# Chunks 1 and 4 in row Pairs ahead of the first down stage, chunk 2's second norm transposed by DMA, eleven half tiles, row copies on VectorE: one change to an adaLN block

## The chip, the cores and the metric

One core of one Trainium2 chip. The metric is the device time of one execution of the program in microseconds (us), median over runs.

## The reference, cut to what matters

An adaLN block on x of 2048 rows by D = 576 columns, bf16: local dilated attention of 32 heads of 18 columns, then a gated MLP of width F = 4608, each behind a layer norm that is scaled and shifted by vectors made from a condition c, and each added to x through a gate.

```python
# sa, ca, ga, sb, cb, gb = the six blocks of silu(c) @ w_mod
h = layernorm(x) * (1 + ca) + sa
q, k, v = split(h @ wqkv)
# row s looks at rows s, s-2, ..., s-14; softmax over these 8, per head
o = softmax((q . k[s - 2w]) * 18**-0.5, over w) . v[s - 2w]
x = x + ga * (o @ wo)
h = layernorm(x) * (1 + cb) + sb
x = x + gb * (((h @ w_gate) * (h @ w_up)) @ w_down)
```

## The kernel before, in words

The rows are cut into eight chunks of 256. The MLP runs over groups of chunks, GROUPS = [[0], [1, 2], [3, 4], [5, 6], [7]] (L42). For each group there is a gate/up stage and then a down stage. Everything else, that is the attention and both norms of later chunks, is threaded between the matmuls of these stages.

*Gate/up.* The 4608 columns are 36 f tiles of 128, loaded in nine blocks of four (`load_wgu`, SP's queue, three rotating buffers). One f tile is a `Pair` (L772): TensorE's 128 rows are used as two halves of 64 contraction rows, the gate product on one half and the up product on the other, and then the halves swap banks. `first` of a Pair is put ahead of `second` of the Pair before it. ScalarE (ACT) evicts both products as u_sb and g_sb, VectorE (DVE) multiplies them into hh (L815 for a half tile, L824 for a full one). In the second gate/up stage (chunks 1 and 2) the first HEAD = 8 f tiles are each split into "f0" (chunk 1's columns) and "f1" (chunk 2's), so that the stage can begin before chunk 2's second norm is ready; the f1 tiles need the mark "h2". A new weight block is asked for at f = 4, 8, ... of the f1 or full tiles.

*Down.* The 36 tiles of hh are multiplied with w_down's blocks (`load_wd`, GpSimd's queue), 128 by 512 and 128 by 64 per row tile, into one bank per row tile and a shared one. Weight blocks 5 and 6 of the first stage are put in prod_t's space (`ld_prods`, L1332).

*Attention.* For each chunk: `a_ln` and its norm, the transposition into hT (on TensorE, or by DMA on SP's queue, `a_td`, L417), modulation by DVE or ACT, q and k (`a_q` unpaired, `qk_pair` L827 as a Pair), v (`a_v` or `v_pair` L850), rows of v written to DRAM scratch vd and read back shifted as vsh (`b_ld`, L475, GpSimd's queue), products of q and shifted k (`b_p`), logits summed per head on TensorE (`b_l`), softmax, weighting and adding (`b_mul`, `b_add`), o into oT (`b_o` on TensorE, `b_od` by DMA), the output projection (`b_w`, L653, unpaired; `w_pair`, L873, as two Pairs). Then the second norm (`b_ln`, `b_norm`) and its transposition into h2T (`b_t`, L680, ten TensorE transposes; `b_td`, L685, two DMA transposes), modulated afterwards (`b_mod`).

A Pair for attention contracts 576 = 4 × 128 + 64 rows; the last 64 must stand in both halves of the partitions. For the weights this is a copy of 64 rows into the other 64: `both_halves` (L1323: wqk 1152 columns, wv 576) and `wo_both` (L870: wo 576), both on GpSimd. For hT and oT it is a doubled last tile: the norms of chunks 3, 5, 6 and 7 also write 64 columns behind the 576 (`both`), and `o_tail` (L550) fills the same columns of o. PAIRED = (3, 5, 7) lists the chunks whose output projection is a Pair.

*What sets the order.* All engines run in the order of the program. That order is worked out when the kernel is built, by `timed` (L893): it goes through the f tiles with a clock of planned times, and after each tile puts in the pieces of several threads whose marks are due, and at most one extra Pair from a list. In the tables `gbg` (L1362) and in `first_down` (L1375), an entry is (TensorE time, DVE time, marks needed, mark given, delay of that mark, call). Around the change, before:

- In the first gate/up stage (chunk 0): extra Pairs are q, k and v of chunk 3; threads are chunk 3's and 4's first norm and the attention of chunks 1 and 2. `both_halves` is called behind the MLP's gate row.
- In the first down stage: chunk 4's ten transposes, chunk 1's ten o transposes, chunk 4's q and k in five groups and v in two, chunk 1's output projection, all unpaired; then chunk 1's second norm (by DMA transposes), chunk 2's values and its output projection.
- In the second gate/up stage: chunk 2's second norm is transposed on TensorE among the f0 tiles; both vsh loads of chunk 3, its residual rows and `wo_both` come first; then chunk 5's norm and chunk 3's and 4's attention.

Of the kernel before, what the change touches and what calls it, by code (L numbers as in the profile page):

```python
# [18 lines left out]
P = 128  # L19
# [22 lines left out]
GROUPS = [[0], [1, 2], [3, 4], [5, 6], [7]]  # L42
PAIRED = (3, 5, 7)


@with_exitstack
def kernel(
# [279 lines left out]
    def transposed(src, dst, cols, vi):  # L327
        n = P * len(cols)
        pA = ps([P, 3, n], BF, "tr_pA")
        pB = ps([P, 2, n], BF, "tr_pB")  # L330
        for m in range(KT):
            d = pA[:, m, :] if m < 3 else pB[:, m - 3, :]
            for c, j in enumerate(cols):
                nc.tensor.transpose(d[:, js(c)], src[:, j, m * P:(m + 1) * P], ident[:])

        def evict(first_on_dve=True):
            for m in range(KT):
                s = pA[:, m, :] if m < 3 else pB[:, m - 3, :]
                modulate(dst(m), s, m, vi + 1, vi, (m < 3) == first_on_dve)
        return evict  # L340
# [81 lines left out]
    def a_t4():  # L422
        a_t(4, False)
        nc.gpsimd.memset(aa[4]["hT"][64:, KF, :], 0.0)

# [49 lines left out]
    def b_ld(i, j):  # L475
        b = bb.setdefault(i, dict(prod={}, vsh={}))
        base = HALO + i * CH + j * P - DIL * (W - 1)
        vsh = vshp.tile([P, W, DH, H], BF, name="vsh")
        vsrc = bass.AP(vd.tensor, vd.offset + base * D, [[D, P], [DIL * D, W], [1, D]])
        b["vsh"][j] = vsh  # L480
        return nc.gpsimd.dma_start(vsh[:].rearrange("p w d h -> p w (d h)"), vsrc)  # L481

# [200 lines left out]


    def b_td(i):  # L685
        ht, o0 = h2_of(i)
        xn = bb.pop(i)["xn"]
        for j in range(ST):
            nc.sync.dma_start_transpose(out=ht[:, :, o0 + j * P:o0 + (j + 1) * P], in_=xn[:, j, :])

# [34 lines left out]
    def values_of(i, nxt=None):  # L725
        r = []
        for j in range(ST):
            r += [(0, 0.75, f"a{i}", "-", 0, lambda j=j, w=w: b_mul(i, j, w)) for w in range(0, W, 2)]
            r += [(0, 0.75, "", "-", 0, lambda j=j: b_add(i, j, 0)), (0, 0.75, "", "-", 0, lambda j=j: b_add(i, j, 1)),
                  (0, 1.2, "", f"o{i}{j}", 0, lambda j=j: b_add(i, j, 2))]  # L730
            if i in PAIRED:
                r.append((0, 0, "", f"O{i}" if j == ST - 1 else "-", 11.0 if i == 7 else 14.0, lambda j=j: b_od(i, (j,))))
# [137 lines left out]
    def wo_both():  # L870
        nc.gpsimd.tensor_copy(wo[64:, KF, :], wo[0:64, KF, :])

# [18 lines left out]
    QKP = [(0, 1), (2, 3), (4,), (5, 6), (7, 8)]  # L891

    def timed(items, extra, threads, slack, busy=0.0):  # L893

        t, dve = 0.0, busy
        done, seq = {f"v{i}": 0.0 for g in GROUPS for i in g[1:]}, []
        done["late"] = 0.0
        extra, threads = list(extra), [list(th) for th in threads]

# [17 lines left out]
        for kind, f, step, own, need in items:  # L917
# [11 lines left out]
            t += step  # L929
        assert not extra, (extra[0][1], t)  # L930
        return seq, [(*p[0:2], p[2] if all(x in names(th) for x in p[2].split()) else "late", *p[3:]) for th in threads for p in th]

# [11 lines left out]

    HEAD = 2 * FB

# [39 lines left out]
    def wgu_spaces():  # L986
        for k, space in ((3, value_space()), (4, value_space()), (8, prod_t)):
# [3 lines left out]

    WD_ASKS = [{0: (7,), 1: (8,), 2: (9,), 7: (10,)},
# [330 lines left out]
    def both_halves():  # L1323
        for w_t, n in ((wqk, 2 * D), (wv, D)):
            nc.gpsimd.tensor_copy(w_t[64:, KF, 0:n], w_t[0:64, KF, 0:n])

# [32 lines left out]
    first.pop(at)  # L1359
    at = [k for k, p in enumerate(first) if p[3] == "o11"][0] + 2  # L1360
    first.insert(at, (0, 0, "o11", "O1", 0, nop))
    gbg = {0: (qkv_of(3, "p17 z3"),  # L1362
               [[(0, 0, "", "-", 0, lambda: (load_wm5(), load_wd(0))), (0, 0, "", "z3", 8.0, nop), (0, 0, "", "w5", 12.0, nop), (0.85, 0, "w5", "-", 0, gb_row), (0, 0, "", "-", 0, lambda: (load_res(2), both_halves()))],
                norm_of(3, "", "", 5) + [(0, 2.5, "", "m4", 0.2, lambda: a_ln(4)), (0, 0, "m4", "r4", 1.0, lambda: aa[4]["rsq"]()),
                                         (0, 0, "r4", "e4", 2.0, lambda: aa[4]["norm"]((0,))), (0, 0, "e4", "n4", 1.6, lambda: aa[4]["norm"]((1,))),
                                         (0, 0, "n4 v3", "x4", 0, nop)],
               first, [(0, 0, "y1", "s1", 0.6, lambda: b_exp(1))]]),
           1: (qkv_of(5, "p37") + wo_of(3),
               [[(0, 0, "", "-", 0, lambda: (loads_v(3), load_res(3), load_res(4), wo_both()))], norm_of(5, "p33", "", 7), second]),
           2: (qkv_of(6, "") + wo_of(5),  # L1370
# [3 lines left out]

    def first_down(late):  # L1375
        def q(g):
            return (0.53 if g == 2 else 1.07, 0, "h4", "-", 0, lambda: a_q(4, g))

        def v(j):
            return (1.2, 0, "h4", "-", 0, lambda: a_v(4, j))  # L1380

        def out_1(first):
            return [(0, 0, "", "o0", 0.4, nop), (0.55, 0, "o0", "o1", 1.9, lambda: b_o(1)), (1.2, 1.35, "o1", "-", 0, lambda: b_w(1, 0)), (1.2, 1.35, "", "x1", 0.5, lambda: b_w(1, 1)),
                    (0, 2.5, "", "s1", 0.7, lambda: b_ln(1)), (0, 0, "s1", "n1", 2.3, lambda: b_norm(1)), (0, 0, "n1", "t1", 9.5, lambda: b_td(1)),
                    (0, 1.0, "t1", "-", 0, lambda: (b_mod(1, (3, 4), False), b_mod(1, (0, 1, 2), True)))]
        assert not {"O1", "x4"} & set(names(late))
        a4 = [(0.6, 0, "", "h4", 1.7, lambda: (a_t4(), load_x(6), ld_prods(0)))]
# [19 lines left out]
    for gi, grp in enumerate(GROUPS):  # L1407
# [15 lines left out]
        else:  # L1423
            left = down(gi, hh, first_down(late) if gi == 0 else next_down(gi, late))
            assert gi == 0 or not left
# [30 lines left out]
```

## Time and profile before

| what | us |
|---|---|
| median of three runs | 539.52 |
| lowest and highest | 539.25 to 539.95 |
| the profiled execution | 541.99 |
| its span | 539.7 |

The profile is of one execution of its own; its span leaves out what lies before the first and behind the last recorded instruction. Its first part gives each engine's busy time, its second the span in 40 slices, its third the DMA queues (q0 are GpSimd's, q1 SP's and ACT's). The chain is followed back from the last instruction to what released each one. In timelines a row is: start, duration, engine, line, operation, output<-input, shapes, count, and in brackets the idle time before it with what ended it.

### The profile page before, as it was taken

How to read it: one execution, taken by the hardware profiler on the slowest of the kernel's cores; microseconds unless marked ns; L12 is line 12 of the kernel's file. 1: busy time of each engine (PE TensorE's matmuls, PEld its weight loads, DVE VectorE, ACT ScalarE, POOL GpSimd, SP SyncE). 2: the span in 40 equal slices, each digit the busy share in tenths (PEclk: the TensorE clock that was granted, in tenths of full speed). 3: DMA queues.
4: the chain of work that ended last, by engine and by line, in shares of the span. 5: the costliest groups of instructions: out<-in, count | busy, mean ns of one | idle time of the engine just before them, and what ended most of it. 6: DMA issues, size and time to landing. Idle time of an engine off the chain costs nothing.

```text
span 539.7 us, 14692 instructions
## 1 busy us (share of the span) xinstructions
PE 531.5 (98%) x6214; PEld 324.0 (60%) x6244; DVE 319.5 (59%) x731; ACT 252.8 (47%) x620; POOL 73.1 (14%) x113
## 2 busy tenths in 40 slices
PE   8999999999999999999999999999999999999997
PEld 4777889756755444555544454555544454558875
DVE  5898797759767788627467797504517733032212
ACT  4866877644656553112655543104555542006630
POOL 8104023112000110111000010110010101110210
PEclk9999999999999999999999999999999999999999
DMA  9999999979863871998445944983396694759731
GB/s 273 292 242 363 346 278 321 322 128 326 279 181 90 237 229 28 264 273 299 130 130 145 302 149 108 238 237 111 94 279 184 158 312 81 233 138 292 259 96 38
DMA packets 94659, 114.47 MB, mean 212 GB/s; under 512 B 27873, under 2 KB 83378, under 8 KB 94466
## 3 DMA queue, kind: packets, MB, share of 16 engines
q1 hardware_dynamic: 82864, 66.92, 45.7%
q0 software_dynamic: 11424, 46.40, 27.5%
q8 instruction: 49, 0.80, 0.7%
q10 hardware_dynamic: 306, 0.21, 0.1%
q14 instruction: 16, 0.13, 0.1%
HBM read 103.07 MB, written 4.74 MB: 200 GB/s over the span
## 4 chain that ended last, share of the span: by engine, by line
PE 97%; DMA 1%; issue 1%; DVE 0%; SPq 0%; ACT 0%
PE pg L770 29%; PE pu L770 23%; PE acc L1007 19%; PE pq L442 4%; PE pq L770 3%; PE accr L1012 3%; PE acc L1062 3%; PE pv L770 2%; PE pv L465 2%; PE lgT L499 2%; PE pw L659 2%; DMA wmA<-in_w_mod_dram 1%; PE pw L770 1%; PE po L614 1%; PE pwj L636 0%
## 5 line engine op out<-in xcount | busy, mean ns | idle before, releaser
L770 PE MATMUL pg<-h2T,wgu 64*128 64x512 bf16 (+1 forms) x1376 | 266.0, 331 | 0.0
L770 PE MATMUL pu<-h2T,wgu 64*128 64x512 bf16 (+1 forms) x1376 | 265.5, 331 | 0.0
L770 PEld LDWEIGHTS <-wgu 64*128 64x128 bf16 x2752 | 136.5, 94 | 93.3
L821 ACT CAST u_sb<-pu 128x512 bf16<-128x512 f32 (+1 forms) x172 | 85.4, 497 | 152.4 <-PE pg L770 150.4
L824 DVE TENSOR_TENSOR hh<-g_sb,u_sb 128x512 bf16<-128x512 bf16 x136 | 59.2, 435 | 114.1 <-ACT g_sb L822 113.1
L822 ACT CAST g_sb<-pg 128x512 bf16<-128x512 f32 (+1 forms) x172 | 86.8, 505 | 0.0
L1007 PEld LDWEIGHTS <-hh 128*128 128x128 bf16 x504 | 49.0, 98 | 59.3 <-issue 1.5
L1007 PE MATMUL acc<-wd,hh 128*128 128x512 bf16 x327 | 84.1, 380 | 0.1
L1012 PE MATMUL accr<-wd,hh 128*128 128x64 bf16 x344 | 62.4, 193 | 0.8
L770 PE MATMUL pu<-h2T,wgr 64*128 64x512 bf16 (+1 forms) x188 | 61.4, 327 | 0.0
L770 PE MATMUL pg<-h2T,wgr 64*128 64x512 bf16 (+1 forms) x188 | 61.4, 327 | 0.0
L1012 PEld LDWEIGHTS <-hh 128*128 128x128 bf16 x504 | 45.8, 98 | 1.2
L175 POOL DMA_DIRECT2D wd<-in_B_w_down_dram x29 | 21.8, 751 | 176.2 <-PE accr L1012 142.0
L548 DVE TENSOR_TENSOR vsh<-vsh,attn 128x1152 bf16<-128x1152 bf16 x56 | 39.7, 750 | 0.0
L487 DVE TENSOR_TENSOR prod_t<-qT,kT 128x1280 bf16<-128x1280 bf16 x36 | 28.2, 817 | 4.5 <-ACT kT L841 2.7
L770 PEld LDWEIGHTS <-wgr 64*128 64x128 bf16 x376 | 19.6, 94 | 15.1 <-issue 2.7
L1007 PE MATMUL acc<-prod_t,hh 128*128 128x512 bf16 x108 | 27.7, 380 | 0.0
L481 POOL DMA_DIRECT2D vsh<-vd x14 | 12.5, 896 | 96.6 <-DVE o_sb L556 76.1
L770 PE MATMUL pq<-hT,wqk 64*128 64x256 bf16 (+1 forms) x360 | 22.9, 259 | 0.0
L442 PE MATMUL pq<-hT,wqk 128*128 128x256 bf16 (+1 forms) x225 | 21.7, 251 | 0.1
L1012 PE MATMUL accr<-prod_t,hh 128*128 128x64 bf16 x112 | 21.6, 193 | 0.2
L325 ACT ACTIVATE h2T<-h2T,modc 128x256 bf16<-128x256 bf16 x12 | 6.5, 591 | 31.4 <-DMA h2T<-xn 31.4
(225 smaller groups left out, 628.3 us busy)
## 6 DMA issues: line engine op xcount, KB each, us to landing
wgu<-in_B_w_gate_dram SPq DMA_DIRECT2D x41, 512.0 KB, 4.8
wgu<-in_B_w_up_dram SPq DMA_DIRECT2D x41, 512.0 KB, 6.5
wd<-in_B_w_down_dram POOLq DMA_DIRECT2D x29, 576.0 KB, 5.2
vsh<-vd POOLq DMA_DIRECT2D x14, 1152.0 KB, 8.8
prod_t<-in_B_w_down_dram POOLq DMA_DIRECT2D x8, 576.0 KB, 5.9
hh<-in_B_w_down_dram POOLq DMA_DIRECT2D x6, 576.0 KB, 6.8
x_t<-in_A_x_dram SPq DMA_DIRECT2D x8, 288.0 KB, 5.3
x_r<-in_A_x_dram SPq DMA_DIRECT2D x8, 288.0 KB, 8.5
```

Of the source, the lines that this page charges most:

```text
L175: return nc.gpsimd.dma_start(wb[:], B_w_down[r0:r0 + FB * P, :].rearrange("(k p) n -> p k n", p=P))
L442: nc.tensor.matmul(pq[:, gi, :], lhsT=wqk[:, kt, m * P:(m + 1) * P], rhs=hT[:, kt, cols], start=(kt == order[0] and not (by_k and gi)), st ...
L481: return nc.gpsimd.dma_start(vsh[:].rearrange("p w d h -> p w (d h)"), vsrc)
L487: nc.vector.tensor_tensor(prod, aa[i]["qT"][:], aa[i]["kT"][:, :, off:off + CH], ALU.mult)
L548: nc.vector.tensor_tensor(v, v, at, ALU.mult)
L770: return nc.tensor.matmul(out, lhsT=lhs, rhs=rhs, start=first, stop=last, skip_group_check=True)
L821: nc.scalar.copy(u[:, c, :], pu)
L822: nc.scalar.copy(g[:, c, :], pg)
L824: return lambda: nc.vector.tensor_tensor(hh[:, f - c:f + 1, :], g, u, ALU.mult)
L1007: nc.tensor.matmul(acc[j][:], lhsT=hh[:, f, js(j)], rhs=wb[:, f % FB, 0:512], start=(f == 0), stop=(f == FT - 1))
L1012: nc.tensor.matmul(accr[:, j, :], lhsT=hh[:, f, js(j)], rhs=wb[:, f % FB, 512:D], start=(f == 0 and j == 0), stop=(f == FT - 1), skip_grou ...
L1062: nc.tensor.matmul(acc[i][:], lhsT=hh[:, f, js(j)], rhs=wb(f)[:, c0:c1], start=(f == 0), stop=(f == FT - 1))
```

## The change

- PAIRED gets chunk 1: its output projection becomes two extra Pairs at the end of the first gate/up stage. Its ten o transposes, and chunk 4's ten hT transposes, are put ahead of them there. `o_tail` runs for chunks 1 and 2.
- Chunk 4's q and k become five extra Pairs behind those, at the end of the first gate/up stage, with no gate/up tile between them (`timed` now also appends what is left of `extra`). Its v becomes two extra Pairs at the head of the second. All five hT tiles are modulated by DVE; its norm, on ACT, is put in four pieces and also writes the 64 columns; the GpSimd memset of hT goes.
- Chunk 2's second norm is transposed by two DMAs on SP, behind the output rows' writes; ACT modulates two tiles and DVE three. The f1 tiles still need "h2".
- HEAD is 11 rather than 8.
- Chunk 3's first vsh load waits for the landing of chunk 2's transposes (`behind`), the second stands behind it on GpSimd's queue.
- The three copies of rows run on VectorE, all at the place of `both_halves`.
- Chunk 5's hT transposes stand behind the request of the fourth weight block of the second gate/up on SP's queue, and chunk 3's logit transposes ahead of it.
- The first down stage asks for its blocks at other steps, and its first two blocks in prod_t wait for the first vsh load of chunk 2.

```diff
-PAIRED = (3, 5, 7)
+PAIRED = (1, 3, 5, 7)
...
-                modulate(dst(m), s, m, vi + 1, vi, (m < 3) == first_on_dve)
+                modulate(dst(m), s, m, vi + 1, vi, first_on_dve == 5 or (m < 3) == first_on_dve)
...
-        xn, rsq, norm = layernorm(lambda j: x[:, j, :], "a", i in (3, 4), i in (3, 5, 6, 7))
+        xn, rsq, norm = layernorm(lambda j: x[:, j, :], "a", i in (3, 4), i >= 3)
...
     def a_t4():
-        a_t(4, False)
-        nc.gpsimd.memset(aa[4]["hT"][64:, KF, :], 0.0)
+        a_t(4, 5)
+        load_x(6)
...
+    tds = {}
+
     def b_td(i):
         ht, o0 = h2_of(i)
         xn = bb.pop(i)["xn"]
         for j in range(ST):
-            nc.sync.dma_start_transpose(out=ht[:, :, o0 + j * P:o0 + (j + 1) * P], in_=xn[:, j, :])
+            tds[i] = nc.sync.dma_start_transpose(out=ht[:, :, o0 + j * P:o0 + (j + 1) * P], in_=xn[:, j, :])
...
     def wo_both():
-        nc.gpsimd.tensor_copy(wo[64:, KF, :], wo[0:64, KF, :])
+        nc.vector.tensor_copy(wo[64:, KF, :], wo[0:64, KF, :])
...
+        for pe, need, mark, make, *_ in extra:
+            assert ready(need), (need, t)
+            seq.append(("pair", make))
+            t += pe
+            done[mark] = t + pe + 1.0
+            fill()
...
-    HEAD = 2 * FB
+    HEAD = 11
...
-    WD_ASKS = [{0: (7,), 1: (8,), 2: (9,), 7: (10,)},
+    WD_ASKS = [{0: (7,), 3: (8,), 5: (9,), 7: (10,)},
...
     def both_halves():
         for w_t, n in ((wqk, 2 * D), (wv, D)):
-            nc.gpsimd.tensor_copy(w_t[64:, KF, 0:n], w_t[0:64, KF, 0:n])
+            nc.vector.tensor_copy(w_t[64:, KF, 0:n], w_t[0:64, KF, 0:n])
...
             r = load_wd(g)
-            if gi:
-                behind(r, wgu_in[gi * NBLK + NBLK - 1])
+            behind(r, wgu_in[gi * NBLK + NBLK - 1] if gi else bb[2]["ld"])
...
-    gbg = {0: (qkv_of(3, "p17 z3"),
+    gbg = {0: (qkv_of(3, "p17 z3") + wo_of(1) + qkv_of(4, "p27")[:5],
...
+               [(0, 2.5, "W11", "S1", 0.7, lambda: b_ln(1)), (0, 0, "S1", "N1", 2.3, lambda: b_norm(1)), (0, 0, "N1", "T1", 9.5, lambda: b_td(1)),
+                       (0, 1.7, "T1", "-", 0, lambda: b_mod(1, (3, 4, 0, 1, 2), True))],
+               first, [(1.15, 0, "o11 n4 v3", "O1", 2.3, lambda: (a_t4(), b_o(1))), (0, 0, "O1", "h4", 0.6, nop)],
+               [(0, 0, "y1", "s1", 0.6, lambda: b_exp(1))], [(0, 0, "", "V2", 52.5, nop)], [(0, 0, "", "W2", 56.5, nop)]]),
+           1: (qkv_of(4, "")[5:] + qkv_of(5, "p37") + wo_of(3),
+               [[(0, 0, "", "h4", 0, nop), (0, 0, "h2", "-", 0, lambda: (load_res(3), load_res(4), behind(b_ld(3, 0), tds[2]), b_ld(3, 1)))], norm_of(5, "p33 M2", "v4 B3", 7), second, [(0, 0, "", "B3", 19.0, nop)]]),
...
-              (0, 2.2, "", "s2", 0.7, lambda: b_ln(2)), (0, 1.5, "s2", "n2", 0.2, lambda: b_norm(2)), (0.55, 1.0, "n2", "-", 0, lambda: b_t(2))]
-        return [a4, out_1(True), late + [(0, 0, "", "a2", 0.0, nop)] + values_of(2) + o2, [q(0), q(1), q(2), q(3), q(4), v(0), v(1)]]
+              (0, 2.2, "", "s2", 0.7, lambda: b_ln(2)), (0, 1.5, "s2", "n2", 0.2, lambda: b_norm(2)), (0, 0, "n2", "T2", 6.0, lambda: b_td(2)),
+              (0, 0, "T2", "M2", 0, lambda: (b_mod(2, (3, 4), False), b_mod(2, (0, 1, 2), True)))]
+        return [[(0, 0, "", "-", 0, lambda: ld_prods(0))]] + parts[:-1] + [parts[-1] + o2]
```

More of the change, by code (lines that the diff above doesn't have):

```diff
@@ L480, in b_ld @@
         b["vsh"][j] = vsh
-        return nc.gpsimd.dma_start(vsh[:].rearrange("p w d h -> p w (d h)"), vsrc)
+        r = nc.gpsimd.dma_start(vsh[:].rearrange("p w d h -> p w (d h)"), vsrc)
+        b.setdefault("ld", r)
+        return r
     def b_p(i, w):
@@ L891 @@
     QKP = [(0, 1), (2, 3), (4,), (5, 6), (7, 8)]
+    parts = []
     def timed(items, extra, threads, slack, busy=0.0):
@@ L897, in timed @@
         done["late"] = 0.0
+        for x in extra:
+            done.pop(x[2], None)
         extra, threads = list(extra), [list(th) for th in threads]
@@ L929, in timed @@
             t += step
-        assert not extra, (extra[0][1], t)
-        return seq, [(*p[0:2], p[2] if all(x in names(th) for x in p[2].split()) else "late", *p[3:]) for th in threads for p in th]
+        for pe, need, mark, make, *_ in extra:
[4 more added lines that the diff above has]
+            fill()
+        parts[:] = [[(*p[0:2], p[2] if all(x in names(th) for x in p[2].split()) else "late", *p[3:]) for p in th] for th in threads]
+        return seq, [p for th in parts for p in th]
     def names(th):
@@ L1349, in gb_row @@
         ld_d1(3)
-    first = attention_of(1, 2)[12:-14]
+    first = attention_of(1, 2)[12:]
+    first.insert(-14, (0, 0, "V2", "-", 0, nop))
+    first.insert(-7, (0, 0, "W2", "-", 0, nop))
     first = [(0, 0, "", "p17", 2.2, nop), (0.75, 0, "p17", "l14", 1.0, lambda: b_l(1, 4)), (0.35, 0, "l14", "t14", 0.3, lambda: b_lt(1))] + first
@@ L1359 @@
     first.pop(at)
-    at = [k for k, p in enumerate(first) if p[3] == "o11"][0] + 2
-    first.insert(at, (0, 0, "o11", "O1", 0, nop))
-    gbg = {0: (qkv_of(3, "p17 z3"),
-               [[(0, 0, "", "-", 0, lambda: (load_wm5(), load_wd(0))), (0, 0, "", "z3", 8.0, nop), (0, 0, "", "w5", 12.0, nop), (0.85, 0, "w5", "-", 0, gb_row), (0, 0, "", "-", 0, lambda: (load_res(2), both_halves()))],
+    gbg = {0: (qkv_of(3, "p17 z3") + wo_of(1) + qkv_of(4, "p27")[:5],
+               [[(0, 0, "", "-", 0, lambda: (load_wm5(), load_wd(0))), (0, 0, "", "z3", 8.0, nop), (0, 0, "", "w5", 12.0, nop), (0.85, 0, "w5", "-", 0, gb_row), (0, 1.0, "", "-", 0, lambda: (load_res(2), both_halves(), wo_both()))],
                 norm_of(3, "", "", 5) + [(0, 2.5, "", "m4", 0.2, lambda: a_ln(4)), (0, 0, "m4", "r4", 1.0, lambda: aa[4]["rsq"]()),
[L1365 to L1369, printed above, removed]
+                                         *[(0, 0, f"r4" if k == 0 else f"e4{k - 1}", f"e4{k}" if k < 3 else "n4", 1.0 if k < 3 else 1.6, lambda k=k: aa[4]["norm"]((k // 2,), (k % 2,))) for k in range(4)]],
+               [(0, 2.5, "W11", "S1", 0.7, lambda: b_ln(1)), (0, 0, "S1", "N1", 2.3, lambda: b_norm(1)), (0, 0, "N1", "T1", 9.5, lambda: b_td(1)),
[4 more added lines that the diff above has]
+               [[(0, 0, "", "h4", 0, nop), (0, 0, "h2", "-", 0, lambda: (load_res(3), load_res(4), behind(b_ld(3, 0), tds[2]), b_ld(3, 1)))], norm_of(5, "p33 M2", "v4 B3", 7), second, [(0, 0, "", "B3", 19.0, nop)]]),
            2: (qkv_of(6, "") + wo_of(5),
@@ L1423 @@
         else:
-            left = down(gi, hh, first_down(late) if gi == 0 else next_down(gi, late))
+            left = down(gi, hh, first_down([th for k, th in enumerate(parts) if th and k != 3] + [parts[3]]) if gi == 0 else next_down(gi, late))
             assert gi == 0 or not left
```

14 lines of the change are left out of this document (2 added, 12 removed).

## The prediction

> **What bounds the kernel now.** I read the busy shares on the page first, then the chain of work that ended last, then the idle entries of the other engines.
>
> ```profile
> span 539.7 us, 14692 instructions
> PE 531.5 (98%) x6214; PEld 324.0 (60%) x6244; DVE 319.5 (59%) x731; ACT 252.8 (47%) x620; POOL 73.1 (14%) x113
> PEclk9999999999999999999999999999999999999999
> PE 97%; DMA 1%; issue 1%; DVE 0%; SPq 0%; ACT 0%
> ```
>
> TensorE is busy for 531.5 of 539.7 us, the chain that ends last is TensorE for 97%, and its granted clock stands at the top digit in all 40 slices. The kernel is therefore a packed list of matmuls, and the price of a change is what it adds to or takes from that list, plus any hole that it opens or closes in it. DVE (59%) and ACT (47%) matter only where TensorE waits for them.
>
> Inside a TensorE-bound span a stall can hide as a matmul run that takes longer than its like. So the next views are the chain's shares by line in four windows: 97 to 110 us (first down stage), 158 to 182 (chunk 5 in the second gate/up), 73.9 to 90 (chunk 3 in the first gate/up), 131 to 134 (chunk 2's second norm).
>
> ```profile
> by line: PE pq L442 37.8%; PE pv L465 16.4%; PE pw L659 16.2%; PE acc L1007 14.9%; PE accr L1012 4.8%; PE oT_pA L576 3.4%; PE pwr L657 2.8%; PE pvr L467 2.5%; issue 1.2%; PE tr_pB L334 0.9%; PE oT_pB L576 0.9%
> ...
> by line: PE pg L770 37.2%; PE pu L770 30.7%; PE pq L770 18.5%; PE pv L770 9.2%; PE lgT L499 5.0%
> ...
> by line: PE pq L770 34.1%; PE pu L770 27.8%; PE pg L770 24.4%; PE pv L770 13.7%; issue 0.2%
> ...
> by line: PE pu L770 40.0%; PE pg L770 39.9%; PE tr_pA L334 14.7%; PE tr_pB L334 7.5%
> ```
>
> Share times window gives microseconds. Unpaired (first line, 13 us): q and k 37.8% = 4.91, v (pv and pvr) 18.9% = 2.46, output projection (pw and pwr) 19.0% = 2.47. As Pairs (second line, 24 us): q and k 18.5% = 4.44, v 9.2% = 2.21. Chunk 3 does the same paired work (third line, 16.1 us) in 34.1% = 5.49, so 1.05 us of it is waiting. The last line (3 us) holds the ten transposes: 22.2% = 0.67.
>
> **The change part by part.**
>
> *Pairing.* Chunk 4's q and k fall from 4.91 to 4.44: −0.47. Its v falls from 2.46 to 2.21: −0.25. Chunk 1's output projection is two Pairs of 288 columns, as v is: 2.47 to 2.21, −0.26. Chunk 1's ten o transposes and chunk 4's ten h transposes are only moved from the first down stage to the end of gate/up: nothing. The q and k Pairs stand back to back there, so ACT must evict each in 0.98; a pair's two evictions take 0.62 to 0.66 (rows 77.83 and 79.64 below). The first output Pair waits for ACT's copies of oT, now with only the transposes and a tile between; that can't be priced from a row and is in the 0.3 below.
>
> *Chunk 2's second norm by DMA.* The ten transposes leave TensorE: −0.67. What it costs is a wait (first rival).
>
> *Eleven half tiles.* Periods of ACT's u_sb evictions, TensorE-paced, half tiles then full ones:
>
> ```profile
> 140.93 0.37 ACT L813 CAST u_sb<-pu 128x256 bf16<-128x256 f32 x1 [0.34 <-PE pg L770]
> 141.91 0.37 ACT L813 CAST u_sb<-pu 128x256 bf16<-128x256 f32 x1 [0.34 <-PE pg L770]
> ...
> 152.53 0.59 ACT L821 CAST u_sb<-pu 128x512 bf16<-128x512 f32 x1 [0.87 <-PE pg L770]
> 154.47 0.58 ACT L821 CAST u_sb<-pu 128x512 bf16<-128x512 f32 x1 [0.87 <-PE pg L770]
> ```
>
> A half tile is 0.98, a full one 1.94; three more split tiles cost 3 × (1.96 − 1.94) = +0.06. ACT and DVE do three more small evictions each, under a TensorE that is the longer one.
>
> *Rows copied by VectorE.* The chain's pieces for the first q/k Pair of chunks 3 and 5, and what stood behind the first on DVE, POOL and ACT:
>
> ```profile
> 74.00 1.06 PE pq L770 x10
> ...
> 158.32 0.55 PE pq L770 x10
> ```
> ```profile
> 62.86 0.42 DVE L824 TENSOR_TENSOR hh<-g_sb,u_sb 128x512 bf16<-128x512 bf16 x1 [1.53 <-ACT g_sb L822]
> ...
> 65.10 0.42 DVE L824 TENSOR_TENSOR hh<-g_sb,u_sb 128x512 bf16<-128x512 bf16 x1 [0.86 <-ACT g_sb L822]
> ...
> 69.38 0.82 DVE L487 TENSOR_TENSOR prod_t<-qT,kT 128x1280 bf16<-128x1280 bf16 x1
> 71.00 2.09 DVE L824 TENSOR_TENSOR hh<-g_sb,u_sb 128x512 bf16<-128x512 bf16 x1 [0.81 <-ACT g_sb L822]
> 73.01 1.70 DVE L323 TENSOR_SCALAR hT<-hT,modc 128x256 bf16<-128x256 bf16 x5
> ```
> ```profile
> 71.63 1.17 POOL L1325 COPY wqk<-wqk 64x1152 bf16<-64x1152 bf16 x1
> 72.71 0.90 POOL L1325 COPY wv<-wv 64x576 bf16<-64x576 bf16 x1
> ```
> ```profile
> 76.88 0.30 ACT L290 ACTIVATE ln_rstda<-ln_mva,eps 128x2 f32<-128x2 f32 x1 [0.72 <-DVE ln_mva L285]
> ...
> 77.83 0.62 ACT L839 CAST qT<-pq 128x256 bf16<-128x256 f32 x2
> ...
> 79.64 0.66 ACT L839 CAST qT<-pq 128x256 bf16<-128x256 f32 x2
> ```
>
> The hh product at 71.00 takes 2.09 where its like take 0.42: it runs beside POOL's copy at 71.63 and ends only at 73.09, so the modulation of chunk 3's hT starts 1.67 late and its q/k Pair, already begun, crawls: 1.06 against 0.55. With no copy on POOL I take that back whole: −0.51. The remaining 0.54 of chunk 3's excess I put down to ACT, which stands 0.72 for DVE's late statistics at 76.88 and then evicts behind time. The statistics come some 1.6 earlier; two 64-column norms of chunk 4 are added on ACT. Between 0 and −0.54 I take −0.25.
>
> The trace has no copy of these rows on DVE. Three are added (1152, 576 and 576 columns), and they stand behind the hh product of 62.86. The nearest rows from above are POOL's two (1.17 and 0.90, and the 0.68 one below): 2.75 together. From below, 0.34 apiece, a 256-column modulation (1.70/5): 1.0. I take 1.2. They delay the last products ahead of chunk 2's logits, which end at 70.20; the logits' matmuls start at 72.2. DVE's idle 0.86 and 0.81 take them up in part, the 2.0 of slack the rest. Price nothing; without that cover, 0.7 at most.
>
> [...]
>
> *Queues.* SP's order around the fourth block's request, and the wd loads:
>
> ```profile
> 140.96 0.37 SPq L158 DMA_DIRECT2D wgu<-in_B_w_gate_dram  x1
> ...
> 146.46 2.60 SPq L420 DMA_TRANSPOSE hT<-xn  x2
> ...
> 149.79 2.46 SPq L517 DMA_TRANSPOSE lg_t<-lgs  x2
> ```
> ```profile
> wgu<-in_B_w_up_dram SPq DMA_DIRECT2D x41, 512.0 KB, 6.5
> wd<-in_B_w_down_dram POOLq DMA_DIRECT2D x29, 576.0 KB, 5.2
> vsh<-vd POOLq DMA_DIRECT2D x14, 1152.0 KB, 8.8
> ```
>
> Chunk 3's logit transposes (2.46 of issuing) now stand ahead of the block's request; their logits' matmuls come some four half tiles before the buffer is free, so SP should be through. Chunk 5's hT goes behind the request and has, as now (146.46 to its Pair at 158.32), some 11 us. The first down stage is shorter and asks for its wd blocks in other steps: by my count of tiles each is still asked for about 10 us ahead of use, against 5.2 to land. Nothing for all three. POOL's two vsh loads wait for h2T, and behind them on POOL stand only loads that are due later.
>
> *Smaller ones.* The unpaired attention work in the first down stage shows 1.2% "issue" (0.16 us in 13); most goes: −0.1. o_tail of chunks 1 and 2 and the memset are DVE work off the path. For new small waits in a list of some 240 moved instructions I add +0.3.
>
> Sum: −0.47 −0.25 −0.26 −0.67 +0.06 −0.51 −0.25 −0.1 +0.3 = **−2.15 us**. It is made against the profiled execution (span 539.7 inside 541.99). Carried over to the runs' median, 539.52, it gives **537.4**.
>
> **The rivals.**
>
> *First: chunk 2's h2T lands after the eleventh half tile (ends slower).*
>
> ```profile
> 126.87 0.81 PE acc L1007 x3
> ```
> ```profile
> 130.46 1.63 DVE L299 TENSOR_SCALAR xn<-x,ln_mvb,ln_rstdb 128x576 bf16<-128x576 bf16 x4
> ...
> 144.00 1.19 DVE L299 TENSOR_SCALAR xn<-x_t,ln_mva,ln_rstda 128x576 bf16<-128x576 bf16 x4
> ```
> ```profile
> 130.48 0.68 POOL L871 COPY wo<-wo 64x576 bf16<-64x576 bf16 x1
> ```
> ```profile
> 111.62 2.60 SPq L689 DMA_TRANSPOSE h2T<-xn  x2
> ```
> ```profile
> L323 DVE TENSOR_SCALAR h2T<-h2T,modc x18: 336/342/346, 123.2 to 459.7; 128x256 bf16<-128x256 bf16 x18
> ...
> DMA to landing us min/median/max: 4.9/6.4/10.3
> ```
>
> Call G the end of the first down stage, 127.68 now. DVE's norms end at 132.09, G + 4.4; without the wo copy of 130.48 beside them they last 1.19 instead of 1.63, so G + 4.0. SP takes 1.3 an issue, so the second transpose goes out near G + 4.8. The first f1 tile is ready to begin after eleven half tiles and the two v Pairs, 10.8 + 2.2, less the 0.4 by which a Pair's first half is put ahead of its predecessor's second: G + 12.6. Three modulations (0.34 each, queued between hh products) need about 1.2 behind the landing. So a landing up to 6.6 after the second issue costs nothing. The twelve transposes of this kind took 4.9 to 10.3, median 6.4; the long ones stood beside gate/up blocks in flight, and here those have landed, with only two wd loads ahead. I expect about 5 and no wait. At 10.3 TensorE stands 3.7, and the result is −2.15 + 3.7 = +1.5: **541.0**. It decides from a landing 9.9 after issue.
>
> [...]
>
> *Second: the fourth gate/up block comes late.*
>
> ```profile
> 128.72 1.76 POOL L481 DMA_DIRECT2D vsh<-vd  x2
> ```
> Its buffer comes free behind the fourth f1 tile, as now, but only seven half tiles and one full one (8.8, less 1.4 for the release behind a second half) then stand before its use: a lead of 7.4. Its up half lands in 6.5 at the median. Chunk 3's two vsh loads, now asked for at G + 1.0 and, at the median's 8.8, landed before the block is requested at G + 13.3, start behind h2T's landing, near G + 10.5, and at 8.8 and more each overlap the request at about G + 19. If they delay the block to 10, TensorE stands 2.6, and the sum is +0.45: **540.0**.
>
> *Third: the holes stay.* The pairing, the transposes and the half tiles are arithmetic (−0.47 −0.25 −0.26 −0.67 +0.06 = −1.6); chunk 3's Pair may instead be late for its DMA transposes or for VectorE's copies, and the dense Pairs at the end of gate/up may wait 0.8 for oT and evictions. Then −0.8: **538.7**.
>
> **How the numbers follow.** Chances: the forecast 0.62 (536.2 to 538.4), the third 0.13, the second 0.11, the first 0.14. The range leaves out less than two in ten: it begins at 536.2 (all of chunk 3's excess regained, −0.29 more; no new waits, −0.3; and 0.6 for holes that I did not find) and ends at 541.0, the first rival at its longest landing. A measurement of this kernel tells about 0.2%, 1.1 us, from no change. Faster by more: the forecast and the mildest of the second, 0.65. Within it: the third and the second as priced, 0.17. Slower: the first and the second with a block later than 11, 0.18.
>
> **What would show it.** Right: hh products near 71 us at 0.42; chunk 3's first q/k piece at 0.55; q and k of chunk 4 at 4.4 by the end of gate/up; the first down stage about 11 us shorter; no TensorE idle at the first f1 tile and at the thirteenth tile (f = 12). Wrong: an idle entry of PE or of ACT's u_sb of over 1 us at either place, released by DMA or by DVE's h2T; a q/k piece over 1; POOL's vsh or SP's block requests held behind a wait.

## The result, and the profile after

The changed kernel takes 538.0 us (median of six runs, 537.48 to 538.79), the kernel before 539.83 beside it (six runs, 539.25 to 540.59): a ratio of 0.9959, 95% interval 0.9948 to 0.9971, or −1.8 us. In another set of runs the same kernel gave 0.9956 (0.9942 to 0.9971). The forecast was −2.15. The page of the profile after, with the rows that answer to those of before:

```profile
span 536.5 us, 14991 instructions
PE 530.2 (99%) x6365; PEld 327.8 (61%) x6365; DVE 319.3 (60%) x748; ACT 251.7 (47%) x629; POOL 70.3 (13%) x109
PEclk9999999999999999999999999999999999999999
PE 97%; DMA 1%; DVE 0%; SPq 0%; issue 0%; ACT 0%
```

TensorE is still the bound: busy for 530.2 of 536.5 us, with the granted clock at the top digit in all 40 slices. The span is shorter by 3.2 us, not by 1.8, and that is the first thing to be careful about. Cutting both traces at the first matmul of each stage gives this (us):

| stage | before | after | difference |
|---|---|---|---|
| setup, until the first gate/up | 49.31 | 48.03 | −1.28 |
| first gate/up | 46.54 | 53.70 | +7.16 |
| first down | 31.76 | 20.76 | −11.00 |
| second gate/up | 82.45 | 84.52 | +2.07 |
| the six stages until the last down | 308.22 | 308.22 | 0.0 |
| last down and what follows | 21.42 | 21.30 | −0.12 |

The setup isn't touched by the change. In the profiled execution of before its chain holds one hole:

```profile
37.10 1.08 issue
```

None of the eleven other profiled executions of this study (the changed kernel's and those of the kernels below) has it; they began the first gate/up between 47.5 and 49.15 us. So the 1.08 belongs to that execution and not to the kernel. The three stages that the change touches make −1.77, close to what the medians say.

The chain's shares in three windows of the changed kernel: chunk 3's Pairs (72.4 to 88.5, again 16.1 us), the end of the first gate/up (90 to 106), the head of the second (122.5 to 128).

```profile
by line: PE pg L774 32.4%; PE pq L774 27.5%; PE pu L774 26.6%; PE pv L774 13.7%
...
by line: PE pq L774 27.7%; PE acc L1021 23.6%; PE pw L774 13.8%; PE pg L774 12.5%; PE pu L774 12.3%; PE accr L1026 2.9%; PE oT_pA L578 2.8%; PE tr_pA L334 2.8%; PE tr_pB L334 1.4%; PE oT_pB L578 0.7%; issue 0.1%
...
by line: PE pg L774 40.9%; PE pv L774 40.1%; PE pu L774 18.5%; PE acc L1021 3.9%
```

Chunk 3's q and k take 27.5% of 16.1 = 4.43 (5.49 before). Chunk 4's take 27.7% of 16 = 4.43 (4.91), chunk 1's output projection 13.8% = 2.21 (2.47), chunk 4's v 40.1% of 5.5 = 2.21 (2.46). VectorE around the copies:

```profile
61.59 0.42 DVE L828 TENSOR_TENSOR hh<-g_sb,u_sb 128x512 bf16<-128x512 bf16 x1 [1.53 <-ACT g_sb L826]
62.03 0.45 DVE L1339 COPY wqk<-wqk 64x1152 bf16<-64x1152 bf16 x1
62.41 0.30 DVE L1339 COPY wv<-wv 64x576 bf16<-64x576 bf16 x1
62.62 0.30 DVE L875 COPY wo<-wo 64x576 bf16<-64x576 bf16 x1
...
69.72 0.42 DVE L828 TENSOR_TENSOR hh<-g_sb,u_sb 128x512 bf16<-128x512 bf16 x1 [0.81 <-ACT g_sb L826]
70.06 1.37 DVE L323 TENSOR_SCALAR hT<-hT,modc 128x256 bf16<-128x256 bf16 x5
```

The copies take 1.05 together. The product that took 2.09 beside GpSimd's copies takes 0.42, and the five modulations behind it 1.37 rather than 1.70.

The place where the first rival would have struck, on SP, VectorE, ACT and TensorE (the second gate/up begins at 122.49: that is the prediction's G):

```profile
126.07 2.54 SPq L693 DMA_TRANSPOSE h2T<-xn  x2
...
141.52 0.50 SPq L158 DMA_DIRECT2D wgu<-in_B_w_gate_dram  x1
```
```profile
133.59 0.28 DVE L819 TENSOR_TENSOR hh<-g_sb,u_sb 128x256 bf16<-128x256 bf16 x1
133.80 0.85 DVE L323 TENSOR_SCALAR h2T<-h2T,modc 128x256 bf16<-128x256 bf16 x3
```
```profile
133.84 1.10 ACT L325 ACTIVATE h2T<-h2T,modc 128x256 bf16<-128x256 bf16 x2
```
```profile
135.07 0.27 PE L774 MATMUL pg<-h2T,wgr 64*128 64x256 bf16 x1
...
141.95 0.27 PE L774 MATMUL pu<-h2T,wgu 64*128 64x256 bf16 x1
142.51 0.28 PE L774 MATMUL pg<-h2T,wgu 64*128 64x256 bf16 x1 [0.29 <-issue]
```

VectorE's three modulations stand behind a product and ACT's two behind an eviction, neither behind a DMA. VectorE's end at 134.65, 12.2 behind the start of the stage, and ACT's at 134.94, 12.45 behind it. The first f1 tile begins at 135.07, so ACT is the later of the two and leaves 0.13 us. TensorE has no idle entry there, nor at the thirteenth tile. Its one hole in the stage is at 142.2, where the next matmul comes 0.56 later instead of 0.11: 0.45 us with the releaser "issue".

### The profile page after: what moved, and what is told of

Read it like the earlier page. It is cut to its first block, busy times and chain, and to the rows that moved or that the text cites. A ratio compares the mean times of both kernels' runs of the same rounds, so it can differ in the third digit from the quotient of the medians.

```text
span 536.5 us, 14991 instructions
## 1 busy us (share of the span) xinstructions
PE 530.2 (99%) x6365; PEld 327.8 (61%) x6365; DVE 319.3 (60%) x748; ACT 251.7 (47%) x629; POOL 70.3 (13%) x109
## 4 chain that ended last, share of the span: by engine, by line
PE 97%; DMA 1%; DVE 0%; SPq 0%; issue 0%; ACT 0%
PE pg L774 29%; PE pu L774 24%; PE acc L1021 20%; PE pq L774 4%; PE pq L442 3%; PE accr L1026 3%; PE acc L1076 3%; PE pv L774 2%; PE pw L774 2%; PE lgT L501 2%; PE pv L465 1%; PE pw L661 1%; DMA wmA<-in_w_mod_dram 1%; PE po L616 1%; PE pwj L638 0%; PE accr L1079 0%
## 5 line engine op out<-in xcount | busy, mean ns | idle before, releaser
L774 PEld LDWEIGHTS <-wgu 64*128 64x128 bf16 x2800 | 140.0, 94 | 90.8 <-issue 0.9
L825 ACT CAST u_sb<-pu 128x512 bf16<-128x512 f32 (+1 forms) x169 | 83.9, 496 | 155.9 <-PE pg L774 150.9
L828 DVE TENSOR_TENSOR hh<-g_sb,u_sb 128x512 bf16<-128x512 bf16 x133 | 56.3, 423 | 109.4 <-ACT g_sb L826 108.5
L1021 PE MATMUL acc<-wd,hh 128*128 128x512 bf16 x344 | 85.7, 380 | 0.0
L826 ACT CAST g_sb<-pg 128x512 bf16<-128x512 f32 (+1 forms) x169 | 84.9, 502 | 0.0
L774 PE MATMUL pu<-h2T,wgr 64*128 64x256 bf16 (+1 forms) x191 | 61.9, 324 | 0.0
L774 PE MATMUL pg<-h2T,wgr 64*128 64x256 bf16 (+1 forms) x191 | 61.9, 324 | 0.0
L774 PE MATMUL pq<-hT,wqk 64*128 64x256 bf16 (+1 forms) x450 | 26.8, 258 | 0.0
L774 PEld LDWEIGHTS <-wqk 64*128 64x128 bf16 x450 | 21.3, 94 | 5.3
```

Source lines behind the costliest of these rows:

```text
L774: return nc.tensor.matmul(out, lhsT=lhs, rhs=rhs, start=first, stop=last, skip_group_check=True)
L825: nc.scalar.copy(u[:, c, :], pu)
L826: nc.scalar.copy(g[:, c, :], pg)
L828: return lambda: nc.vector.tensor_tensor(hh[:, f - c:f + 1, :], g, u, ALU.mult)
L1021: nc.tensor.matmul(acc[j][:], lhsT=hh[:, f, js(j)], rhs=wb[:, f % FB, 0:512], start=(f == 0), stop=(f == FT - 1))
```

## The experiments

Each ratio is to the kernel before, run beside the experiment on the same chip; stage times are from the trace, cut as in the table above.

**Copies alone.** In the kernel before:

```diff
-            nc.gpsimd.tensor_copy(w_t[64:, KF, 0:n], w_t[0:64, KF, 0:n])
+            nc.vector.tensor_copy(w_t[64:, KF, 0:n], w_t[0:64, KF, 0:n])
...
-        nc.gpsimd.tensor_copy(wo[64:, KF, :], wo[0:64, KF, :])
+        nc.vector.tensor_copy(wo[64:, KF, :], wo[0:64, KF, :])
```

> The kernel before with one part of the change: the three copies of 64 rows run on VectorE, at the places where GpSimd had them. Theory (the copies on GpSimd held VectorE's product at 71.0 for 2.09 us, and all of chunk 3's excess follows from that): the product near 71 takes 0.42, chunk 3's q and k Pairs 4.44 in place of 5.49, the first gate/up stage 45.5 in place of 46.5, the whole about -1.05 us (ratio 0.998). Rival 1 (half of the excess is ACT's own backlog): the first Pair falls to 0.55, the others keep 0.5 of excess, -0.5 us. Rival 2 (VectorE's copies cost what they save): no change of the stage.

Measured: 539.84 against 540.62 us, ratio 0.9990 (0.9975 to 1.0005), so the time alone doesn't tell; the trace does. The chain's shares from 72 to 88.1 us, and TensorE's one hole in the stage, and ACT where it had stood 0.72 for VectorE's statistics (76.88 in the prediction):

```profile
by line: PE pg L770 34.3%; PE pq L770 27.5%; PE pu L770 26.0%; PE pv L770 13.7%
```
```profile
68.89 0.27 PE L770 MATMUL pu<-h2T,wgu 64*128 64x256 bf16 x1 [0.41 <-issue]
```
```profile
74.43 0.31 ACT L290 ACTIVATE ln_rstda<-ln_mva,eps 128x2 f32<-128x2 f32 x1
```

Chunk 3's q and k take 27.5% of 16.1 = 4.43: all of the 1.05 is gone. The stage is 46.04 rather than 45.5 because of that hole (0.56 more from matmul to matmul than the 0.11 around it). ACT no longer waits for the statistics. The theory holds in this trace; that half of the excess is ACT's own does not.

**Copies back on GpSimd**, in the changed kernel, all three at the place of `both_halves` (the diff above, reversed).

> The changed kernel with the three copies of rows back on GpSimd, all at the place of both_halves. Theory: the VectorE product beside them is held until they end, chunk 3's q and k Pairs rise from 4.43 to about 5.5 (up to 6.1, as the copy of wo is there too), the first gate/up stage from 53.7 to 54.8 to 55.4, the whole +1.05 to +1.7 us against the changed kernel, so 0.1 to 0.8 faster than before. Rival (ACT's backlog is the larger part and ACT now has other work): +0.5. Rival 2 (the copies matter nothing here): no change against the changed kernel.

Measured: 539.64 against 540.62, ratio 0.9982 (0.9971 to 0.9993). The first gate/up takes 55.34. The shares from 72 to 88.1, then VectorE, GpSimd and ACT:

```profile
by line: PE pq L774 32.7%; PE pu L774 24.5%; PE pg L774 21.7%; PE pv L774 13.7%; DVE hT L323 7.6%; issue 0.5%
```
```profile
69.85 0.42 DVE L828 TENSOR_TENSOR hh<-g_sb,u_sb 128x512 bf16<-128x512 bf16 x1 [1.26 <-ACT g_sb L826]
70.19 3.52 DVE L323 TENSOR_SCALAR hT<-hT,modc 128x256 bf16<-128x256 bf16 x5
```
```profile
70.72 1.17 POOL L1339 COPY wqk<-wqk 64x1152 bf16<-64x1152 bf16 x1
71.81 0.70 POOL L1339 COPY wv<-wv 64x576 bf16<-64x576 bf16 x1
72.46 0.66 POOL L875 COPY wo<-wo 64x576 bf16<-64x576 bf16 x1
```
```profile
75.87 0.29 ACT L290 ACTIVATE ln_rstda<-ln_mva,eps 128x2 f32<-128x2 f32 x1 [0.72 <-DVE ln_mva L285]
```

Here the product got through before the copies began, and the five modulations behind it were held instead: 3.52 for 1.37. VectorE now stands on the chain itself, and ACT waits 0.72 for the statistics again. Chunk 3's q and k run to 5.61 (counted from matmul to matmul), +1.18; the other 0.45 by which the stage is longer than 53.70 is a hole at 68.87 with the releaser "issue", at the place of the copies-alone hole. So it isn't the one product that suffers: here the modulations did, and the loss is what the theory said.

**Copies doubled.** In the changed kernel the two copies of `both_halves` run twice.

```diff
             nc.vector.tensor_copy(w_t[64:, KF, 0:n], w_t[0:64, KF, 0:n])
+            nc.vector.tensor_copy(w_t[64:, KF, 0:n], w_t[0:64, KF, 0:n])
```

> The changed kernel with the copies of the rows of wqk and wv run twice on VectorE (0.75 us more there). Theory (VectorE's idle time and the slack of 2 us ahead of chunk 2's logits cover them): the first gate/up stage stays at 53.7, within 0.1; no change of the whole. Rival (VectorE is the bound in this part of the stage): the stage gets up to 0.75 longer.

Measured: 537.91 against 540.73, ratio 0.9954 (0.9938 to 0.9969); the first gate/up 53.85, chunk 3's q and k 4.43. Of the 0.75 us that the second copies add on VectorE at most 0.15 reaches the stage (53.70 without them), a little more than the 0.1 that was allowed. VectorE has room for nearly all of it, and a price of nothing is right to within that.

**Chunk 2's transposes on TensorE again.** Chunk 3's vsh loads then have no landing to wait for.

```diff
-... behind(b_ld(3, 0), tds[2]), b_ld(3, 1)))], ...
+... b_ld(3, 0), b_ld(3, 1)))], ...
...
-... (0, 0, "n2", "T2", 6.0, lambda: b_td(2)),
-              (0, 0, "T2", "M2", 0, lambda: (b_mod(2, (3, 4), False), b_mod(2, (0, 1, 2), True)))]
+... (0.55, 1.0, "n2", "M2", 0, lambda: b_t(2))]
```

> The changed kernel with chunk 2's second norm transposed by TensorE again (ten transposes, evicted by ACT and VectorE), eleven half tiles kept, chunk 3's vsh loads behind the mark of h2 alone. Theory: the second gate/up stage gets 0.67 longer (84.5 to 85.2) and nothing else moves, +0.67 us against the changed kernel (about -1.2 against before). Rival (the DMA way costs elsewhere, by a late fourth weight block or held queues): the stage gets longer by clearly less than 0.67, or shorter.

Measured: 538.8 against 540.62, ratio 0.9971 (0.9959 to 0.9983). The second gate/up takes 84.83. The changed kernel's 84.52 has the 0.45 hole; without it 84.07, and four other executions that leave this stage as it is (with GpSimd's copies, the copies doubled, chunk 4's transposes apart, and the changed kernel again) had 83.95 or 83.96. So the transposes cost 0.8 to 0.9, of which 0.67 is their own matmuls and the rest is isolated by no run, and no other stage gets longer by sending them through the DMA queues.

**Eight half tiles.**

```diff
-    HEAD = 11
+    HEAD = 8
...
-... (0, 0, "n2", "T2", 6.0, lambda: b_td(2)),
+... (0, 0, "n2", "T2", 2.5, lambda: b_td(2)),
```

> The changed kernel with eight half tiles in place of eleven (and the planned landing of chunk 2's transposes set shorter, so that the order can be made). Theory (the three extra half tiles only buy time for the transposes): f1 is wanted 2.95 us sooner, h2T is modulated 12.2 us behind the start of the stage, so TensorE stands about 2.4 at the first f1 tile; less 0.06 of three tiles; the stage 84.5 to 86.8, the whole +2.3 us against the changed kernel and 0.5 slower than before. Rival (the landing follows its neighbours, not a clock: with other loads moved it comes sooner): a wait under 1 us, and no loss against the changed kernel.

Measured: 544.31 against 540.62, ratio 1.0074 (1.0051 to 1.0097); the second gate/up takes 90.73. The expectation was right in sign and wrong in its working. TensorE, and VectorE at the landing and later:

```profile
134.01 0.27 PE L774 MATMUL pg<-h2T,wgr 64*128 64x256 bf16 x1 [1.11 <-ACT h2T L325]
...
157.72 1.42 PE L774 MATMUL pq<-hT,wqk 64*128 64x256 bf16 x10 [3.13 <-DVE hT L323]
```
```profile
132.88 0.86 DVE L323 TENSOR_SCALAR h2T<-h2T,modc 128x256 bf16<-128x256 bf16 x3 [1.20 <-DMA h2T<-xn]
...
155.33 1.00 DVE L529 TENSOR_REDUCE mx<-lg_t 128x64 f32<-128x512 bf16 x1 [5.01 <-DMA lg_t<-lgs]
```

At f1 TensorE waits 1.11, not 2.4: with the modulations planned sooner they start on the landing (132.88, 9.8 behind the start), not 11.3 behind it. The rest came from the shorter planned landing, which rearranged SP's queue: chunk 3's logit transposes went behind chunk 5's hT and three loads, VectorE stood 5.01 for them, and TensorE 3.1 for the modulations of hT queued behind. This run therefore doesn't isolate the half tiles; the next does.

**Ten half tiles**, one character (`HEAD = 10`), which leaves SP's queue as it is.

> The changed kernel with ten half tiles in place of eleven, nothing else: SP's order and VectorE's up to the f1 tiles stay. Theory (h2T is modulated 12.2 us behind the start of the stage, the first f1 tile could now begin at 11.6): TensorE stands 0.5 to 0.6 at the first f1 tile, the clock stays up as the wait is short; the fourth weight block gains 1 us of lead; the stage 84.05 - 0.02 + 0.55 = 84.6, the whole +0.5 us against the changed kernel. Rival (the eleventh tile is not needed): no wait and 84.0. Second rival (eleven is a compromise and the fourth block was the tighter end): shorter than with eleven, under 84.0.

Measured: 538.49 against 540.37, ratio 0.9969 (0.9957 to 0.9982), beside 0.9956 for eleven in the same set; the intervals overlap, so the trace has to tell. VectorE, ACT and TensorE (the stage begins at 123.61):

```profile
134.92 0.85 DVE L323 TENSOR_SCALAR h2T<-h2T,modc 128x256 bf16<-128x256 bf16 x3
```
```profile
134.96 1.10 ACT L325 ACTIVATE h2T<-h2T,modc 128x256 bf16<-128x256 bf16 x2
```
```profile
136.11 0.27 PE L774 MATMUL pg<-h2T,wgr 64*128 64x256 bf16 x1 [0.73 <-ACT h2T L325]
```

VectorE's modulations again end 12.2 behind the start and ACT's 12.45, with no DMA in their brackets. TensorE goes on at 136.11, right behind ACT's end at 136.06; it waits 0.73, and the stage is 84.84, 0.9 over 83.95. So in this order eleven is the smallest count that closes the gap, and what closes last is ACT's two modulations, not the landing. Their place is given by the planned landing (6.0 in the table): with 2.5 planned, in the run before, they began on the landing, 9.8 behind the start. Whether ten or fewer would do with a plan in between was not tried.

**Chunk 3's vsh loads early.**

```diff
-... [(0, 0, "", "h4", 0, nop), (0, 0, "h2", "-", 0, lambda: (load_res(3), load_res(4), behind(b_ld(3, 0), tds[2]), b_ld(3, 1)))], ...
+... [(0, 0, "", "h4", 0, lambda: loads_v(3)), (0, 0, "h2", "-", 0, lambda: (load_res(3), load_res(4)))], ...
```

> The changed kernel with chunk 3's two vsh loads no longer behind the landing of chunk 2's transposes, but at the head of the second gate/up stage, as in the kernel before. Theory (these loads and the transposes share the transfer engines, and where GpSimd's loads run SP's queue gets little): the second transpose lands 9 to 10 behind its issue rather than 5.4, h2T is ready some 4 later, TensorE stands 3 to 4 at the first f1 tile, the stage goes from 84.5 to about 88, the whole +3.5 us against the changed kernel, 1.5 slower than before. Rival (the order of the loads is of no matter): the transposes land in 5 to 6.5 and the stage stays within 0.5 of 84.5.

Measured: 544.83 against 540.73, ratio 1.0088 (1.0065 to 1.0112); the second gate/up takes 90.93, 7.0 over 83.95. SP's queue, the first matmul of f1, and a row of h2T's tile page from 118 to 142 us (the two transposes):

```profile
126.04 7.09 SPq L693 DMA_TRANSPOSE h2T<-xn  x2
```
```profile
139.86 0.37 PE L774 MATMUL pg<-h2T,wgr 64*128 64x256 bf16 x1 [4.65 <-ACT h2T L325]
```
```profile
DMA to landing us min/median/max: 10.6/11.3/11.9
```

The two transposes take 7.09 even to issue, and land 10.6 and 11.9 behind their issue (5.4 and 5.5 in the changed kernel): without this order of the loads the DMA way loses more than the whole change gains. But a wait of 4.65 doesn't explain 7.0. The windows of the same trace, in microseconds from the start, with TensorE's busy time, the granted clock, the DMA share and GB/s:

```profile
core 0: us, PE busy (x), PEclk, DMA share, GB/s
134.00:135.00 1.00, 1.00 (x23) 1.00 0.50 172
...
136.00:137.00 1.00, 0.00 (x0) 1.00 1.47 125
137.00:138.00 1.00, 0.00 (x0) 0.84 1.31 176
138.00:139.00 1.00, 0.00 (x0) 0.50 1.08 353
...
143.00:144.00 1.00, 1.00 (x24) 0.50 0.00 0
144.00:145.00 1.00, 1.00 (x19) 0.75 0.00 0
```

Some 2.5 us into the idle time the granted clock falls to half (at 137.7), and it stays there until 144.5, 4.6 behind the first matmul. From 140.02 on the steps from one matmul of pg to the next are 0.21 to 0.24 rather than 0.11. Half the speed for 4.6 us loses 2.3: 4.65 + 2.3 = 6.95. With eight half tiles the wait of 3.1 was followed by the same: the clock stood at 0.50 from 158.8, a microsecond after TensorE had gone on, to 162.1. The two stretches at half last 6.8 and 3.4 us; what sets where they begin and end no run isolates. After the wait of 1.1 in the run with eight half tiles the clock stayed at 1.00, up to 158; the execution with the wait of 0.73 has a mean granted clock of 0.999.

**Chunk 4's transposes apart from chunk 1's.**

```diff
-... [(1.15, 0, "o11 n4 v3", "O1", 2.3, lambda: (a_t4(), b_o(1))), ...
+... [(0.6, 0, "n4 v3", "Q4", 0, a_t4), (0.55, 0, "o11", "O1", 2.3, lambda: b_o(1)), ...
```

> The changed kernel with chunk 4's ten transposes put in as soon as their own marks are due, no longer together with chunk 1's ten o transposes. Theory (the holes of 0.28 us at the end of the first gate/up stage are a bank that ACT frees late, because four banks are taken at once): the stage goes from 53.70 to about 53.4 to 53.5, the whole -0.2 us, less than a timing can tell. Rival (the holes come with any switch between Pairs and full-height matmuls): 53.7 or, with one more switch, 53.8.

Measured: 540.25 against 540.73, ratio 0.9996 (0.9983 to 1.0010); the first gate/up takes 55.58, 1.9 longer. ACT and VectorE there:

```profile
93.75 0.63 ACT L522 ACTIVATE dd<-dd 128x512 f32<-128x512 f32 x1 [3.17 <-DVE dd L530]
94.28 0.35 ACT L825 CAST u_sb<-pu 128x256 bf16<-128x256 f32 x1
```
```profile
90.38 1.05 DVE L323 TENSOR_SCALAR hT<-tr_pA,modc 128x256 bf16<-128x256 bf16 x3 [0.33 <-PE tr_pA L334]
91.34 0.72 DVE L323 TENSOR_SCALAR hT<-tr_pB,modc 128x256 bf16<-128x256 bf16 x2
91.98 1.01 DVE L529 TENSOR_REDUCE mx<-lg_t 128x64 f32<-128x512 bf16 x1
```

Both the theory and its rival missed. One tile sooner, the transposes put their five modulations ahead of chunk 2's maximum on VectorE; ACT, whose next instruction is the exponential of that, stands 3.17, and the eviction of u_sb queued behind it comes only at 94.28. TensorE stands idle for 1.29 of the two microseconds from 93 (busy 0.41 and 0.30 of them), with the granted clock at 1.00. The changed kernel's own stage is 0.36 longer than its parts add up to: of its +7.16 the terms −1.06 (chunk 3), +2.21, +4.43 and +1.22 (the twenty transposes, counted from matmul to matmul) leave that. Only half of it shows as a hole, 0.29 us from one matmul to the next at 92.31 where the steps around it are 0.11. Whether it comes from the banks stays open.

**Unpaired at the new places.** Chunk 1's output projection and chunk 4's q, k and v run as `b_w`, `a_q` and `a_v` where the change has Pairs.

```diff
+    class Solo:
+        def __init__(self, run):
+            self.run = run
+        def first(self):
+            self.run()
+        def second(self):
+            return nop
...
-... lambda hf=hf: w_pair(i, hf), 1.15) ...
+... lambda hf=hf: w_pair(i, hf) if i > 1 else Solo(lambda: b_w(i, hf)), 1.15) ...
...
-... qk_pair(n, ms))[1]))
+... qk_pair(n, ms) if n != 4 else Solo(lambda: a_q(4, k)))[1]))
...
-... lambda: v_pair(n, 0)), ... lambda: v_pair(n, 1))]
+... lambda: v_pair(n, 0) if n != 4 else Solo(lambda: a_v(4, 0))), ... lambda: v_pair(n, 1) if n != 4 else Solo(lambda: a_v(4, 1)))]
```

> The changed kernel with chunk 1's output projection and chunk 4's q, k and v as unpaired matmuls again, at the places where the change put them. Theory (the pairing is worth its arithmetic): output projection +0.26 and q, k +0.47 in the first gate/up stage (53.7 to 54.4), v +0.25 in the second (84.5 to 84.8), the whole +1.0 us against the changed kernel, 0.8 to 0.9 faster than before. Rival (the Pairs' swaps and evictions eat the gain): under +0.3.

Measured: 540.03 against 540.73, ratio 0.9995 (0.9980 to 1.0010). The first gate/up takes 54.87, the second 84.62. The shares from 94 to 104 and from 124 to 130:

```profile
by line: PE pq L442 50.2%; PE pw L661 21.6%; PE pu L774 11.3%; PE pg L774 9.1%; PE pwr L659 5.0%; PE acc L1032 4.3%; PE accr L1037 0.3%
...
by line: PE pv L465 39.0%; PE pg L774 32.2%; PE pu L774 18.5%; PE acc L1032 7.2%; PE pvr L467 5.4%
```

q and k 5.02, output projection 26.6% = 2.66, v 44.4% of 6 = 2.66: +1.49 over the Pairs, and by the stages +1.17 and +0.55 (over 84.07), 1.7 in all. That is more than the 0.98 of arithmetic: between gate/up Pairs an unpaired group takes 2.66 where it took 2.47 and 2.46 in the down stage. Where the difference comes from no run isolates. Moving this work into gate/up is only worth it because it is paired there: unpaired, the ratio to the kernel before is 0.9995.

**The changed kernel again.**

> The changed kernel itself once more, for its time and for its hole of 0.45 us with the releaser issue at 142 us. Theory (such holes belong to one execution, not to the order): no hole at that place, the second gate/up stage 84.0 to 84.1, first gate/up 53.7; the whole about 2 us faster than before (ratio 0.996). Rival (it belongs to the order, for example a late queue): the hole is there again at the same matmul and the stage is 84.5.

Measured: 538.18 against 540.37, ratio 0.9956 (0.9942 to 0.9971). The second gate/up takes 83.95, with no hole at 142; but the first takes 54.85, and its hole is the one that the copies-alone and the GpSimd runs had:

```profile
69.55 0.27 PE L774 MATMUL pu<-h2T,wgu 64*128 64x256 bf16 x1 [0.97 <-issue]
```

So a hole with the releaser "issue" comes in some executions, at one of a few places, and costs 0.4 to 1.1. The changed kernel's two traces have it at two different places, so it doesn't belong to the order. What makes it stays open.

## Why the prediction was right, point by point

The trace's terms, without the one hole, make −2.3 (7.16 − 11.00 + 1.62 − 0.12), the medians −1.8 and −2.2; the forecast was −2.15. With the measured sizes of chunk 3's term and of the new waits the forecast's own sum would be −2.4, so that the medians lie so near −2.15 owes something to luck: two errors and the holes of single executions are in them.

- *Pairing, −0.98*: right to 0.01 by the shares after. Unpaired at the same places the work costs 1.7 more.
- *Transposes, −0.67, and half tiles, +0.06*: right. The stage without the hole is +1.5 to +1.6, which is v's 2.21 − 0.67 + 0.06. By the run with the transposes on TensorE they are worth 0.8 to 0.9.
- *Rows copied by VectorE*: that GpSimd's copies hold VectorE's work beside them was right (a product of 2.09 beside them, of 0.42 without; five modulations of 3.52 beside them, of 1.37 without); how they hold it no run shows. One size was wrong. The first Pair's −0.51 came. "The remaining 0.54 of chunk 3's excess I put down to ACT, … Between 0 and −0.54 I take −0.25" is the step that failed: all of it went (1.05 in place of 0.76), in the changed kernel and with the copies alone. ACT was late only because VectorE's statistics were: its wait of 0.72 for them went with the copies alone and came back with GpSimd's, so the one cause had paid for all. VectorE's copies take 1.05 (1.2 taken) and, by the doubled ones, cost at most some 0.15.
- *New waits, +0.3*: 0.36 at the end of the first gate/up, and in the profiled execution the 0.45 hole at 142, which another execution does not have. The −0.1 for "issue" in the first down stage is isolated by no run.
- *First rival*: the second transpose was to go out at G + 4.8 and to land in about 5; the pair was issued from G + 3.6 to G + 6.1 and landed in 5.4 and 5.5, and VectorE and ACT started without a wait for it at G + 11.3. That a landing decides was wrong for this order: the modulations stand behind other work that ends later. The forecast priced VectorE's three alone; ACT's two end last, and the margin is the 0.13 that they leave. Nor did only the long landings of before stand beside gate/up blocks: those of 5.0, 5.4 and 5.1 (issued at 217.3, 232.7 and 453.9) had such blocks in flight too. The rival's price was too low too: it counted the wait alone, and with each of the two waits over 3 us in these runs came a stretch at half the clock (4.65 of wait, 7.0 of time).
- *Second rival*: the block was requested at G + 19.0, as reckoned, and TensorE shows no wait, but it was near. The up half's load was issued at 142.07; its row and the first matmul on it in the changed kernel's trace:

```profile
wgu<-in_B_w_up_dram SPq DMA_DIRECT2D x1, 512.0 KB, 7.2
```
```profile
149.49 0.38 PE L774 MATMUL pu<-h2T,wgu 64*128 64x512 bf16 x1
```

  It was there at about 149.3, 0.2 us ahead of its use.
- *Third rival*: the holes at chunk 3 did not stay.
- *Which execution*: the sum was carried to the median and not to the span; the span's −3.2 would have been misread.

## What to carry to other kernels

Where a packed engine does the same work twice, compare the two pieces of its chain: here the longer one (5.49 against 4.44) hid a wait, and two small copies on GpSimd cost more (1.05 us by the trace) than nine Pairs (0.98) or ten transposes (0.67) saved. Transposing by DMA took 0.8 to 0.9 us off TensorE here, but the loads around it had to be moved as well (7.0 us lost with two of them left in their place), and enough independent tiles had to be found to cover the landing and the queues of the engines that work on what landed (a wait of 0.73 with ten, none with eleven). Cut the trace by stages before reading a span's difference: a third of this one was a hole in a part that the change didn't touch.

## What the runs showed of the hardware that was not expected

- Waits of TensorE of 1.1 us (eight half tiles, the first f1 tile) and 1.3 (chunk 4's transposes apart) left the granted clock at 1.00; the execution with a wait of 0.73 (ten half tiles) has a mean of 0.999. In the two executions with waits of 3.1 and 4.65 (eight half tiles, vsh loads early) it stood at 0.50 for 3.4 and 6.8 us, and the wait of 4.65 came with a stage 7.0 longer. The forecast priced its rivals by the wait alone.
- Beside GpSimd's copies VectorE's five modulations of hT took 3.52 us in place of 1.37 (copies back on GpSimd, against the changed kernel).
- VectorE copied 64 rows of 1152 columns in 0.45 us and of 576 in 0.30 (the changed kernel), GpSimd in 1.17 and 0.66 to 0.90 (the kernel before and the run with the copies back on GpSimd).
